# Reordering the builds between the token sums and the channel products of an attention-and-mixer kernel, and its fifth block product

## The chip, the cores and the metric

The kernel runs on one core of a Trainium2 chip. The metric is the device time of one execution in microseconds; three runs of the kernel before gave 585.57, 586.85 and 587.18 us, a median of 586.85. The engines are TensorE (PE: matmuls, with its weight loads, PEld), VectorE (DVE), ScalarE (ACT), GpSimd (POOL) and SyncE (SP), which issues most of the DMAs.

## What is computed

A decay-weighted linear attention over blocks of 64 positions feeds an MLP mixer. Cut to what matters (B = 4, H = 8, S = 768, D = 64; 256 hidden token features, 1536 hidden channel features):

```python
def _attn_ref(q, k, v, lam):
    ...
    for b in range(nb):
        intra = np.einsum('bhic,bhjc->bhij', qb, kb) * Dmask[None]
        intra = np.einsum('bhij,bhjd->bhid', intra, vb)
        inter = np.einsum('bhid,bhde->bhie', qb * lam_pow[None], kv_state)
        out[:, :, sl] = intra + inter
        kv_state = lam_block[None, :, None, None] * kv_state + np.einsum('bhsd,bhse->bhde', kb_dec, vb)
    return out

def _moe_ref(x, w_tok1, w_tok2, w_ch1, w_ch2):
    xt = x.transpose(0, 2, 1)
    h = np.maximum(xt @ w_tok1, 0.0) @ w_tok2
    u = x + h.transpose(0, 2, 1)
    h2 = np.maximum(u @ w_ch1, 0.0) @ w_ch2
    return u + h2
```

The weights arrive as 64-bit floats and are narrowed on the chip.

## The kernel before

**Precision.** Every matmul of the mixer is done three times with operands split into a high part (rounded) and a low part (the remainder): high × high, low × high, high × low. A split is a cast on ACT and a subtraction on POOL or DVE. Narrowing a piece of 64-bit weights is five steps (`narrow`, lines 377 to 395): one on ACT (L382) and four on DVE (L383, L386, L389, L392).

**Attention and token mixing** share one loop over 16 pairs of heads (lines 620 to 704). The token mixing of batch entries 0 to 2 is laid between the attention steps; `take` says how many of the groups each step gets. What is in the list `waiting` is given out by `later`, a few at a time, and `later(99)` empties it. Behind the loop come the last four groups (two token sums of entry 2, two hidden groups of entry 3; lines 713 and 714), then the token sums of entry 3 in four pairs (`token_out_pair`, lines 739 to 742). A pair fills two PSUM banks, and there are two such double banks, so a pair waits until DVE has added the pair before the last (L472).

**Channel mixing** is a list of 24 units, a group of 256 hidden channels (of six) for one batch entry each. First come all groups for the entries 0 and 1, alternating, then the groups backwards for the entries 2 and 3. The first matmul of a unit is a product of 2 × 2 blocks with seven products instead of eight (`mixing`, lines 775 to 825). Its moving operands are made from the four quadrants of u in `build` (line 557): B11, B21 and B22 are quadrants, T1 to T4 come from differences (`t1` to `t4`, DVE). Each operand is split (`part`): the high part by ACT (L582), the low part by DVE if it is named in `on_vector`, else by POOL (L584). `first` holds the operands of entry 0, `parts` those of entry 1. The weights' seven operands are made in `split_c1` (line 525) by eight steps: splits (ACT L374, POOL L375) and four differences on DVE (L534 to L537).

The seven products stand in the order m1, m6, m2, m7, m5, m4, m3. `m1` and `m2` add up in bank `pa`, `m6` and `m7` in `pb`, `m5` and `m3` in `pc`, and `m4` uses `pd`. ACT copies `pa` to `s1` (L788), DVE makes `u2` (L793) and `u3` (L806) from `pb`, `c22` from `pc` (L811), `c21` from `pd` (L817) and `c12` from `pc` (L822). So m7 waits until `u2` has been read from `pb`, and m3 until `c22` has been read from `pc`. The hidden blocks 22, 21 and 12 then go through a relu and a cast on ACT (L771, L772) and a subtraction on POOL (L773); block 11 goes through ACT (L799) and DVE (L800).

The second matmul of a unit is given out as four output pairs (0 to 3, `out_pair`, L835 and L850) in the unit behind it. Pairs 0 and 1 read the hidden blocks 11 and 21, pairs 2 and 3 the blocks 12 and 22. They use the same two double banks in turn. The order of products and pairs in a unit is written out by hand:

```python
    SLOTS = ("m1", "m6", 0, 1, "m2", "m7", 2, "m5", "m4", 3, "m3")
```

**Background work.** `run` (line 1010) counts a product as 6 and a pair as 12. `background(n)` (line 918) lists what else unit n has to do, each with a count from which it is due: weight pieces (`piece_steps`: 0 and 1 belong to the first matmul, 2 and 3 to the second), the steps of `split_c1`, operand builds, fetches of the next 64-bit piece (SP) and `save`, which writes a finished weight group to DRAM with six DMAs (L904), from where the second half of the units gets it back. The raw pieces use two buffers in turn (0 and 2 one, 1 and 3 the other).

All five engines take their instructions in the order in which the code issues them.

Of the kernel before, what the change touches and what calls it, by code (L numbers as in the profile page):

```python
# [22 lines left out]
def kernel(  # L23
# [40 lines left out]
    waiting = deque()  # L64

    def later(n):
        n += len(waiting) > 5
        for _ in range(min(n, len(waiting))):
            waiting.popleft()()
# [25 lines left out]
    NI = len(pairs)  # L95
# [99 lines left out]
    n = 1  # L195
# [177 lines left out]
    def split(hi, lo, src):  # L373
        nc.scalar.copy(out=hi, in_=src)  # L374
        nc.gpsimd.tensor_sub(out=lo, in0=src, in1=hi.bitcast(F32))  # L375
# [146 lines left out]
    def narrow_piece(raw, a, sg):  # L522
        return narrow(raw.rearrange("p (n two) -> p n two", two=2), a, sg)
# [18 lines left out]
    def split_c2(to, i, a):  # L542
        c2h, c2l = to[4:]
        return lambda: split(c2h[:, i - 2], c2l[:, i - 2], a.bitcast(F32))
# [55 lines left out]
    weights = {}  # L600
# [19 lines left out]
    for i in range(-2, NI):  # L620
        if 0 <= i + 1 < NI:
            scores(i + 1)
            scale_q(i + 1)
        if i >= 0:
            outputs(i, 0)
        place = state(i + 1) if 0 <= i + 1 < NI else None
        work = [groups.popleft() for _ in range(take.get(i, 0))]
        if i == NI - 1:
            work.pop(0)()
        if i >= 0:  # L630
            outputs(i, 1)
        if i + 2 < NI:
            turn_q(i + 2)
        if i + 2 < NI:
            if 0 < i + 2 < NP:
                masks(i + 2)
            turns = [(turn_k, 0), (turn_k, 1)] if i + 2 < NKD else []
            if i + 2 < NQ:
                turns += [(turn_q_rows, 0), (turn_q_rows, 1)]
            if i == -2:  # L640
                turns.sort(key=lambda x: x[1])
            for f, g in turns:
                f(i + 2, g)
        if place:
            place()
        later(0 if i == NI - 1 else 1 if work else 2)
        n = early.get(i, len(work) // 4)
        cuts = [0, n, max(n, (3 * len(work) + 1) // 4 if len(work) > 2 else len(work) // 2), len(work)]
        for n in range(3):
            for f in work[cuts[n] : cuts[n + 1]]:  # L650
                f()
                later(2 if len(work) < 3 else 1)
            if n < 2 and i >= 0:
                turn_back(i, n)
                later(1 if work else 2 + n)
            if n == 0 and i + 2 < NI:
                scale_k(i + 2)
        if i == -1:
            load_w1(0)
        if 0 <= i + 3 < NI and i >= -1:  # L660
            load_v(i + 3)
        if i == -1:
            load_w1(1)
        if i + 4 < NI:
            load_kq(i + 4)
        if i == -1:
            load_w1(2)
        if i == 1:
            load_w2()
        if 0 <= i < 3:  # L670
            convert_w1(i)
        if 2 <= i < 4:
            convert_w2(i - 2)
        if i == 3:
            convert_w2(2)
        if i == 5:
            weights[0] = group_tiles(0, False)
            w, w3 = words(2), words(3)
            load_piece(0, 0, w[:, 0:1024])
        if i == 6:  # L680
            load_piece(0, 1, w[:, 1024:2048])
            load_piece(0, 2, w3[:, 1024:2048])
            waiting.extend(narrow_piece(w[:, 0:1024], w3[:, 0:512], w[:, 2048:2560]))
        if i == 7:
            waiting.extend(narrow_piece(w[:, 1024:2048], w3[:, 512:1024], w[:, 2560:3072]))
            waiting.extend(split_c1(weights[0], w3[:, 0:512], w3[:, 512:1024], nc.gpsimd))
            load_piece(0, 3, w3[:, 2048:3072])
        if i == 9:
            waiting.extend(narrow_piece(w3[:, 1024:2048], w3[:, 0:512], w3[:, 512:1024]))
            waiting.append(split_c2(weights[0], 2, w3[:, 0:512]))  # L690
        if i == 10:
            homes[0] = {"B11": (up, None, 1), "B21": (up, None, 1), "T2": (kp, "kn", 2), "T1": (kp, "qn", 2)}
            homes[0] |= {"B22": (kp, "kr", 2), "T3": (kp, "kT", 2), "T4": (kp, "qT", 2)}
            first = build(0, 0, on_vector=("T2", "T1"))
            waiting.extend([first["B11"], first["B21"]])
            waiting.extend(narrow_piece(w3[:, 2048:3072], w3[:, 1024:1536], w3[:, 1536:2048]))
            waiting.append(split_c2(weights[0], 3, w3[:, 1024:1536]))
        if i == 11:
            later(99)
        if i == 13:  # L700
            waiting.extend(first[x] for x in ("t1", "t2", "T2", "T1"))
        if i == NI - 1:
            waiting.extend(first[x] for x in ("t3", "T3", "t4", "T4", "B22"))
    later(99)
    att.close()
    ch = ctx.enter_context(tc.tile_pool(name="ch", bufs=1, reuse_waits="tile"))
# [3 lines left out]
    def temp_of(nm):  # L710
        return cp.tile([P, SB], F32, tag="tmp", bufs=5, name=nm)

    for _ in range(4):
        groups.popleft()()
    p1.close()
    cp = ctx.enter_context(tc.tile_pool(name="cp", bufs=1, side="right", reuse_waits="tile"))
    cs = cp.tile([P, 2560], U32, tag="cs", name="cs")
    narrowed = [cs[:, n * 512 : (n + 1) * 512] for n in range(5)]
    raws = {}

    def fetch(to, x):
        raws[x] = hidp.tile([P, 1024], U32, tag=("hh0", "hl0")[x % 2], name=f"raw{to}{x}")
        load_piece(to, x, raws[x])

    def piece_steps(x):
        return narrow_piece(raws[x], narrowed[x], narrowed[4])

    fetch(1, 0)
    fetch(1, 1)
    steps = {}  # L730
    parts = build(1, 1, on_vector=("T2",))
    pa, pb = piece_steps(0), piece_steps(1)
    order = [
        [parts["t1"], parts["B11"], pa[0], pa[1]],
        [parts["t2"], pa[2], parts["B21"], pa[3]],
        [parts["T2"], pa[4], lambda: fetch(1, 2)],
        [parts["T1"]],
    ]
    for n, fs in enumerate(order):
        token_out_pair(B - 1, n // 2, 2 * (n % 2))  # L740
# [172 lines left out]
        f = cs.bitcast(F32)  # L913
        return [f[:, n * 2 * SB : (n + 1) * 2 * SB].rearrange("p (t s) -> p t s", t=2) for n in range(3)]

    SLOTS = ("m1", "m6", 0, 1, "m2", "m7", 2, "m5", "m4", 3, "m3")

    def background(n):

# [3 lines left out]
        def add(when, *fs):  # L923
            ev.extend((when, f) for f in fs)

        if n == 0:
            c1, pb = steps["c1"], piece_steps(1)
            add(12, pb[0], pb[1], pb[2], c1[0])
            add(36, parts["t3"])
            add(36, parts["T3"])  # L930
            add(36, pb[3], pb[4], lambda: fetch(1, 3))
            add(42, c1[1], parts["t4"])
        if n == 1:
            c1, pa = steps["c1"], piece_steps(2)
            add(6, parts["T4"])
            add(24, c1[2], c1[3], c1[4], c1[5], c1[6], pa[0])
            add(36, parts["B22"])
            add(36, pa[1], pa[2], c1[7])
            add(60, pa[3], pa[4], lambda: fetch(2, 0))
            add(72, split_c2(weights[1], 2, narrowed[2]))  # L940
            add(84, lambda: save(0))
        if 1 < n < NP1 - 1:
            to = g + 1
            if n % 2 == 0:
                pa = piece_steps(3)
                add(12, pa[0], pa[1], pa[2])
                add(24, pa[3], pa[4])
                if n < NP1 - 2:
                    add(24, lambda: fetch(to, 1))
                add(36, split_c2(weights[g], 3, narrowed[3]))  # L950
                if n < NP1 - 2:
                    pb = piece_steps(0)
                    weights[to] = group_tiles(to, to % 2)
                    steps["c1"] = c1 = split_c1(weights[to], narrowed[0], narrowed[1], nc.vector)
                    add(36, pb[0])
                    add(48, pb[1], pb[2])
                    add(72, pb[3], pb[4], lambda: fetch(to, 2))
                    add(84, c1[0])
            else:
                c1, pa, pb = steps["c1"], piece_steps(1), piece_steps(2)  # L960
                add(6, pa[0], pa[1], pa[2])
                add(12, pa[3], pa[4], c1[1], lambda: fetch(to, 3))
                add(36, c1[2], c1[3], c1[4], c1[5], c1[6])
                add(48, c1[7], pb[0], pb[1], pb[2])
                add(72, pb[3], pb[4], split_c2(weights[to], 2, narrowed[2]))
                if to < NG - 1:
                    add(72, lambda: fetch(to + 1, 0))
                if to - 1 < NG - 2:
                    add(84, lambda: save(to - 1))
# [25 lines left out]
        if NP1 + 1 <= n < NP1 + 9:  # L995
            x = n - NP1 - 1
            add(36, lambda: store(x // 4, x % 4))
        if n >= NU - 2:
            x = 2 * (n - NU + 2)
# [25 lines left out]
    for n in range(1, NU):  # L1025
        run(n, [x if isinstance(x, str) else (n - 1, x) for x in SLOTS])
    ytags = deque(("hh1", "hl1"))
# [45 lines left out]
```

## Time and profile before

| What | Value |
|---|---|
| the profiled execution | 586.22 us |
| its span, first to last instruction | 584.4 us |
| mean granted clock of PE | 0.993 |
| first product of unit 0 | at 186.98 us |
| attention and token mixing, before that | 187 us |
| the 24 units and what follows them | 397 us |

The profile is of one execution. A row of a timeline gives the start, the duration, the engine, the line of the kernel, the operation, output and inputs by the names of the tiles, and in square brackets how long the engine had been idle and what it waited for. Several engines work at once, so a row's duration counts towards the end only where another engine waits for it. Starts on one engine may lie up to 0.1 us ahead of the end of the row before, because the instructions are pipelined.

### The profile page before, as it was taken

The page shows a single profiled execution, that of the slowest core. Times are in us where ns is not written, and L with a number is a line of the kernel's source. Part 1 is how long each engine was busy: PE and PEld are TensorE (multiplying, and loading weights), DVE is VectorE, ACT ScalarE, POOL GpSimd, SP SyncE. Part 2 cuts the span into 40 slices and gives each one's busy share as a digit, 9 for nine tenths or more (in the row PEclk, how much of TensorE's full clock was granted, in tenths as well). Part 3 has the DMA queues.
Part 4 walks back from the last instruction along what each step waited for, and adds up shares of the span by engine and source line. Part 5 has one row for each costly group of instructions (what it writes and reads, how often), then busy time and mean ns, then how long its engine had stood idle before and what let it go on. Part 6 is the DMA issues. An engine that isn't in the chain of part 4 may idle for free.

```text
span 584.4 us, 10656 instructions
## 1 busy us (share of the span) xinstructions
PE 558.2 (96%) x4234; PEld 541.1 (93%) x4234; DVE 404.1 (69%) x598; ACT 214.5 (37%) x426; POOL 229.6 (39%) x204
## 2 busy tenths in 40 slices
PE   5998999999999879999999998999999999999995
PEld 4888898999998879999999998999999999999994
DVE  4797887787767887878878888874554454454554
ACT  3564432444244443343444354542212222222221
POOL 6675641745316663345345363541112222222110
PEclk9998999999999989999999999999999999999999
DMA  9999999896002144171727200002434353540237
GB/s 186 255 240 187 179 219 182 157 165 114 2 20 90 37 151 156 42 300 37 271 73 268 75 0 1 0 1 38 144 100 140 97 146 97 153 100 1 40 49 128
DMA packets 176593, 67.81 MB, mean 116 GB/s; under 512 B 163616, under 2 KB 166816, under 8 KB 176544
## 3 DMA queue, kind: packets, MB, share of 16 engines
q1 hardware_dynamic: 173200, 66.05, 46.1%
q10 hardware_dynamic: 3344, 1.09, 0.8%
q8 instruction: 33, 0.54, 0.4%
q14 instruction: 16, 0.13, 0.1%
HBM read 49.29 MB, written 17.83 MB: 115 GB/s over the span
## 4 chain that ended last, share of the span: by engine, by line
PE 81%; DVE 9%; DMA 3%; ACT 3%; issue 2%; POOL 1%; SPq 1%; ACTq 0%; DVEq 0%
PE po L835 30%; PE pc L760 8%; PE pb L760 8%; PE pa L760 7%; PE ph L447 6%; PE pu L484 4%; PE xT L323 4%; PE pd L760 4%; PE sc L299 3%; PE xT L333 3%; DMA vn<-in_v_dram 1%; DMA qn<-in_q_dram 1%; DVE uT L850 1%; PE xp L355 1%; PE kv L265 1%
## 5 line engine op out<-in xcount | busy, mean ns | idle before, releaser
L850 DVE TENSOR_TENSOR uT<-po,uT 128x768 f32<-128x768 f32 x94 | 89.7, 954 | 68.3 <-PE po L835 68.1
L773 POOL TENSOR_TENSOR h22l<-c,h22h 128x384 fp32r<-128x384 f32 x24 | 26.1, 1086 | 166.6 <-ACT h22h L772 166.6
L771 ACT ACTIVATE c<-c 128x384 f32<-128x384 f32 x72 | 37.8, 526 | 128.2 <-DVE c L811 91.3
L286 POOL COPY stb<-sv 64x320 f32<-64x320 f32 x32 | 26.6, 833 | 44.7 <-DVE sv L273 43.8
L773 POOL TENSOR_TENSOR h12l<-c,h12h 128x384 fp32r<-128x384 f32 x24 | 25.1, 1048 | 33.6 <-PE pa L760 19.7
L323 PE MATMUL xT<-a,vn 128*64 128x128 f32 x384 | 37.0, 285 | 1.3 <-ACT uT L340 1.0
L340 ACT COPY uT<-xT 128x384 f32<-128x384 f32 x32 | 15.3, 478 | 56.2 <-PE xT L333 56.2
L793 DVE TENSOR_TENSOR u<-pb,s 128x384 f32<-128x384 f32 x24 | 13.4, 557 | 29.7 <-PE pb L760 19.2
L307 DVE TENSOR_TENSOR a<-sc,mask 128x768 f32<-128x768 f32 x32 | 29.1, 949 | 5.9 <-PE sc L299 5.7
L799 ACT ACTIVATE h11h<-pa 128x384 fp32r<-128x384 f32 x24 | 11.7, 486 | 57.8 <-PE pa L760 57.8
L333 PE MATMUL xT<-qs,stb 128*64 128x128 f32 x320 | 31.8, 277 | 0.0
L447 PE MATMUL ph<-xhi,w1h 128*128 128x256 f32 x96 | 28.2, 294 | 0.8 <-DVE uT L489 0.5
L375 POOL TENSOR_TENSOR c1l<-cs,c1h 128x512 fp32r<-128x512 f32 x15 | 19.6, 1320 | 22.4 <-ACT c1h L374 22.4
L323 PEld LDWEIGHTS xT<-a,vn 128*64 128x64 f32 x384 | 22.6, 139 | 5.5 <-ACT uT L340 2.3
L447 PE MATMUL ph<-xhi,w1l 128*128 128x256 f32 x96 | 27.1, 282 | 0.0
L447 PE MATMUL ph<-xlo,w1h 128*128 128x256 f32 x96 | 27.1, 282 | 0.0
L773 POOL TENSOR_TENSOR h21l<-c,h21h 128x384 fp32r<-128x384 f32 x24 | 26.1, 1088 | 1.8 <-ACT h21h L772 1.0
L299 PE MATMUL sc<-qT,kT 64*128 64x128 f32 x384 | 26.3, 284 | 0.2 <-ACT qT L237 0.2
L299 PEld LDWEIGHTS sc<-qT,kT 64*128 64x128 f32 x384 | 23.3, 192 | 3.3 <-issue 1.8
L364 DVE TENSOR_TENSOR xlo<-xp,xhi 128x384 fp32r<-128x384 f32 x32 | 17.7, 552 | 11.4 <-ACT xhi L363 11.3
L252 POOL TENSOR_TENSOR qs<-qT,lamp 128x640 f32<-128x640 f32 x16 | 25.3, 1583 | 0.3
L835 PE MATMUL po<-h12h,c2h 128*128 128x384 f32 x64 | 21.8, 341 | 0.0
(271 smaller groups left out, 1894.7 us busy)
## 6 DMA issues: line engine op xcount, KB each, us to landing
raw<-in_moe_w_ch_dram SPq DMA_DIRECT2D x20, 512.0 KB, 3.9
vn<-in_v_dram SPq DMA_DIRECT2D x16, 384.0 KB, 5.4
kn<-in_k_dram SPq DMA_DIRECT2D x30, 192.0 KB, 4.5
out_dram<-y SPq DMA_DIRECT2D x110, 48.0 KB, 1.8
qn<-in_q_dram SPq DMA_DIRECT2D x44, 96.0 KB, 3.3
kr<-in_k_dram SPq DMA_DIRECT2D x32, 96.0 KB, 2.9
dc1h<-c1h SPq DMA_DIRECT2D x4, 768.0 KB, 5.4
dc1l<-c1l SPq DMA_DIRECT2D x4, 768.0 KB, 6.7
```

Source lines behind the costliest of these rows:

```text
L252: nc.gpsimd.tensor_mul(out=qss[i], in0=qTs[i][:, P:].rearrange("p (c i) -> p c i", i=P), in1=lamp[:, p, None, :].broadcast_to([P, NC - 1, P]),
L286: nc.gpsimd.tensor_copy(out=st[r, :, h, :], in_=sv[r].rearrange("p (e c) -> p c e", c=NC - 1))
L299: nc.tensor.matmul(out=sc[h][:, c * P : (c + 1) * P], lhsT=kTs[i][r, cs], rhs=qTs[i][r, cs], start=True, stop=True,)
L307: nc.vector.tensor_mul(out=a, in0=pair.rearrange("p h (c i) -> p h c i", i=P), in1=mask[:, 2 * p : 2 * p + 2, None, :].broadcast_to([P, 2, ...
L323: nc.tensor.matmul(out=xT[h * D : (h + 1) * D, cs], lhsT=vns[i][:, h, c, :], rhs=weights_of[i, g, h][:, cg, :], start=(cg == 0), stop=False,)
L333: nc.tensor.matmul(out=xT[h * D : (h + 1) * D, cs], lhsT=st[:, c - 1, h, :], rhs=qss[i][:, c - 1, :], start=False, stop=(cg == 2),)
L447: nc.tensor.matmul(out=ph, lhsT=w[:, c, fs], rhs=x[:, c], start=(i == 0), stop=(i == 3 * NC - 1))
L760: nc.tensor.matmul(out=to, lhsT=w[:, t], rhs=x[:, t], start=(start and i == 0), stop=(i == 5), skip_group_check=not start,)
L771: nc.scalar.activation(src, src, AF.Relu)
L773: nc.gpsimd.tensor_sub(out=hl, in0=src, in1=hh.bitcast(F32))
L835: nc.tensor.matmul(out=to, lhsT=w[:, jj, t * P : (t + 1) * P], rhs=h, start=(i == 0), stop=(i == 3 * JG - 1))
L850: nc.vector.tensor_add(out=ub, in0=po, in1=ub)
```

## The change

Four things are altered, and no work is added or left out.

- In every unit but the first, the fifth product stands directly behind the seventh, ahead of output pair 2.
- The builds t3, T3, t4, T4 and B22 of the first operand no longer come at the end of the attention loop; they stand between the last four groups of token work, and their low parts move from POOL to DVE. B11 and B21 of the second operand come up from the pairs of token sums to the same place. T3 of the second operand moves to DVE.
- The steps of weight piece 0, piece 1 and the second operand's remaining builds are spread over the pairs and the units 0 and 1 in another order.
- Weight piece 2 of group 1, with the fetch behind it and its split, moves from unit 1 to the beginning of unit 2. Its fetch then stands behind `save(0)` on SP's queue.

```diff
-            first = build(0, 0, on_vector=("T2", "T1"))
+            first = build(0, 0, on_vector=("T1", "T2", "T3", "T4", "B22"))
...
-        if i == NI - 1:
-            waiting.extend(first[x] for x in ("t3", "T3", "t4", "T4", "B22"))
...
-    for _ in range(4):
+    parts = build(1, 1, on_vector=("T2", "T3"))
+    order = [[first["t3"], parts["B11"]], [first["T3"]], [first["t4"], parts["B21"]], [first["T4"], first["B22"]]]
+    for fs in order:
         groups.popleft()()
+        for f in fs:
+            f()
...
-        return narrow_piece(raws[x], narrowed[x], narrowed[4])
+        return [lambda k=k: narrow_piece(raws[x], narrowed[x], narrowed[4])[k]() for k in range(5)]
...
-    parts = build(1, 1, on_vector=("T2",))
-    pa, pb = piece_steps(0), piece_steps(1)
+    pa = piece_steps(0)
     order = [
-        [parts["t1"], parts["B11"], pa[0], pa[1]],
-        [parts["t2"], pa[2], parts["B21"], pa[3]],
-        [parts["T2"], pa[4], lambda: fetch(1, 2)],
-        [parts["T1"]],
+        [parts["t1"], pa[0]],
+        [parts["t2"], pa[1]],
+        [pa[2], parts["T2"], parts["T1"]],
+        [pa[3], pa[4], lambda: fetch(1, 2)],
     ]
...
-    SLOTS = ("m1", "m6", 0, 1, "m2", "m7", 2, "m5", "m4", 3, "m3")
+    SLOTS = ("m1", "m6", 0, 1, "m2", "m7", "m5", 2, "m4", 3, "m3")
...
         if n == 0:
             c1, pb = steps["c1"], piece_steps(1)
-            add(12, pb[0], pb[1], pb[2], c1[0])
-            add(36, parts["t3"])
-            add(36, parts["T3"])
-            add(36, pb[3], pb[4], lambda: fetch(1, 3))
-            add(42, c1[1], parts["t4"])
+            add(12, pb[0], pb[1], c1[0])
+            add(24, pb[2])
+            add(36, parts["t3"], parts["T3"])
+            add(42, pb[3], pb[4], lambda: fetch(1, 3), c1[1])
         if n == 1:
-            c1, pa = steps["c1"], piece_steps(2)
-            add(6, parts["T4"])
-            add(24, c1[2], c1[3], c1[4], c1[5], c1[6], pa[0])
-            add(36, parts["B22"])
-            add(36, pa[1], pa[2], c1[7])
-            add(60, pa[3], pa[4], lambda: fetch(2, 0))
-            add(72, split_c2(weights[1], 2, narrowed[2]))
+            c1 = steps["c1"]
+            add(12, parts["t4"])
+            add(24, parts["T4"], c1[2], c1[3], c1[4], c1[5])
+            add(36, c1[6], parts["B22"])
+            add(48, c1[7])
             add(84, lambda: save(0))
         if 1 < n < NP1 - 1:
             to = g + 1
             if n % 2 == 0:
+                if n == 2:
+                    pc = piece_steps(2)
+                    add(6, *pc, lambda: fetch(2, 0), split_c2(weights[1], 2, narrowed[2]))
                 pa = piece_steps(3)
```

## The prediction

> **What bounds the kernel now.** I read the page first, then the waits of TensorE (PE), then windows and the chain of waits at the places which those named, and last the timelines of the engines there.
>
> ```profile
> span 584.4 us, 10656 instructions
> ...
> PE 558.2 (96%) x4234; PEld 541.1 (93%) x4234; DVE 404.1 (69%) x598; ACT 214.5 (37%) x426; POOL 229.6 (39%) x204
> ```
>
> PE is busy for 558.2 of 584.4 us, so only its holes can be won: no matmul is added or removed. The profiled execution took 586.22 us around this span; the median of the three runs, 586.85, is 0.63 above it, and I carry differences over unchanged. The columns of the next view are total us, times, longest.
>
> ```profile
> PE pc L760 <- DVE c L811: 6.2, 3, 3.9
> ...
> PE pb L760 <- DVE u L793: 1.7, 1, 1.7
> PE pu L467 <- DVE uT L472: 1.4, 1, 1.4
> ```
>
> All three wait for VectorE (DVE) to empty a PSUM bank: the third product (into `pc`) for `c22`, the seventh for `u2`, a pair of token sums for the sums two pairs earlier. The hole of 3.9 us stands at the end of unit 1, and it costs more than itself (the windows' columns are length, busy time of PE, PEld, DVE, ACT and POOL, granted clock, DMA share and GB/s; the chain's start and length):
>
> ```profile
> 190.00:195.00 5.00, 3.35 (x19) 3.08 (x18) 4.38 (x8) 0.87 (x3) 0.72 (x1) 1.00 0.18 61
> ...
> 215.00:220.00 5.00, 4.92 (x21) 4.95 (x22) 1.98 (x4) 4.45 (x9) 3.89 (x4) 0.71 1.04 421
> ```
>
> ```profile
> 215.08 2.26 PE pc L760 x6
> 217.34 1.36 PE pa L760 x6
> ...
> 233.51 1.06 PE pa L760 x6
> ...
> 235.63 4.16 PE po L835 x24
> ```
>
> A product takes 1.06 us and two output pairs 4.16, so a unit without a hole is 7 × 1.06 + 2 × 4.16 = 15.74 us. Behind the hole the clock is 0.71, and two products take 2.26 + 1.36 instead of 2.12: 1.5 us more. Against no waits at all, 3.9 + 1.5 + 1.7 + 1.4, and 6.2 − 3.9 = 2.3 in the other two waits on `c22`, make 10.8 us: the most that can be won.
>
> **What makes DVE late.**
>
> ```profile
> 179.24 1.84 POOL L584 TENSOR_TENSOR B11l<-uT,B11h 128x768 fp32r<-128x768 f32 x1
> ...
> 171.72 0.95 DVE L574 TENSOR_TENSOR th<-uT 128x768 f32<-128x768 f32 x1
> ...
> 180.08 1.81 DVE L574 TENSOR_TENSOR th<-uT 128x768 f32<-128x768 f32 x1
> ...
> 173.46 1.01 DVE L489 TENSOR_TENSOR uT<-pu,uT 128x384 f32<-128x384 f32 x2
> 173.68 1.86 POOL L584 TENSOR_TENSOR T3l<-th,T3h 128x768 fp32r<-128x768 f32 x1 [12.46 <-issue]
> ```
>
> The same difference takes 0.95 us alone, and 1.81 when it begins while GpSimd (POOL) works: it ends 181.89, which is 0.81 behind POOL's end at 181.08. So a DVE instruction on SBUF alone waits out a POOL one; DVE's additions from PSUM at 173.46 did not. This decides every step below.
>
> **Part 1: the first operand's builds among the token sums.** T3, T4 and B22 leave POOL (3 × 1.86 us) for DVE (3 × 0.95), behind token sums instead of ahead of them; B11 and B21 of the second operand come up from the pairs to between them, still on POOL.
>
> ```profile
> 170.73 0.48 ACT L363 CAST xhi<-xp 128x384 fp32r<-128x384 f32 x1 [0.17 <-PE xp L355]
> 172.70 0.84 ACT L582 CAST T3h<-th 128x768 fp32r<-128x768 f32 x1 [1.49 <-DVE th L574]
> ...
> 171.41 0.33 PE L484 MATMUL pu<-w2l,hh 128*128 128x384 f32 x1
> ...
> 176.93 0.34 PE L467 MATMUL pu<-w2h,hh 128*128 128x384 f32 x1
> ...
> 176.72 0.42 DVE L452 SCALAR_TENSOR_TENSOR hl<-ph,hh 128x256 fp32r<-128x256 f32 x1 [2.25 <-ACT hh L451]
> ...
> 184.79 0.44 PE L467 MATMUL pu<-w2h,hh 128*128 128x384 f32 x1 [1.45 <-DVE uT L472]
> ```
>
> In the new order: ScalarE (ACT) casts B11h from 171.2 to 172.0, and POOL has B11l until 173.9. DVE adds the token sum (171.8 to 172.3), so t3 comes just behind POOL and ends 174.7; next sum 175.2; the cast of T3 (0.84) ends 175.6, T3l 176.6, `hl` 176.9. POOL takes B21l (176.8 to 178.6), t4 waits it out: 179.4; second `hl` 179.7, cast of T4 180.2, T4l 181.2, B22l 182.1. Only then comes the first pair's addition, until 183.0. The third pair needs that bank; PE, which starts the pairs at 176.93 as now, is there at 181.1 (two pairs at 2.08). A new wait of 1.9 us, in place of the 1.45 at the fourth pair, which starts at 185.1 against 184.79: no gain. Should t4 or t3 come ahead of POOL (0.1 to 0.2 us decide), the addition ends at 182.2 or 181.4.
>
> ```profile
> 187.28 1.84 POOL L584 TENSOR_TENSOR T1l<-th,T1h 128x768 fp32r<-128x768 f32 x1 [3.70 <-ACT T1h L582]
> 187.33 2.60 DVE L584 TENSOR_TENSOR T2l<-tl,T2h 128x768 fp32r<-128x768 f32 x1
> ...
> 191.33 0.54 DVE L793 TENSOR_TENSOR u<-pb,s 128x384 f32<-128x384 f32 x1
> ...
> 191.92 0.45 PE L760 MATMUL pb<-T3h,c1h 128*128 128x384 f32 x1 [1.65 <-DVE u L793]
> ...
> 196.22 0.33 PE L760 MATMUL pa<-B11h,a11h 128*128 128x384 f32 x1
> ```
>
> From the end of that addition DVE's line to `u2` is, by starts 0.08 us ahead of the end before: t1, sum and t2 at 0.87, the piece's first step 0.35, a sum 0.87, a step 0.6, 4.4 us in all (the steps' 0.41 and 0.69 stand in a fence below); there T2l and POOL's T1l meet. If T1l is first, as at 187.28, T2l ends at 7.1, and a sum, two steps and `u2` follow: 9.4. If T2l is first, T1l ends at 7.1, the sum runs beside it, and only the two steps and `u2` follow: 8.6. The seventh product of unit 0 begins between 181.4 + 8.6 = 190.0 and 183.0 + 9.4 = 192.4; I take 191.4, nearest the row of now, 191.92. **Gain 0.5 us** (−0.5 to +1.9). The fifth, fourth and third product follow; unit 1 begins 4.2 us later, at 195.6 (now 196.22).
>
> **Part 2: unit 1.** It loses piece 2 (five steps, its split, a fetch) and T3's products on POOL; t4 and T4 move into it from unit 0's end and unit 1's start.
>
> ```profile
> 204.08 2.05 DVE L534 TENSOR_TENSOR cs<-cs 128x256 f32<-128x256 f32 x1 [0.71 <-POOL c1l L375]
> 206.16 0.43 DVE L535 TENSOR_TENSOR cs<-cs 128x256 f32<-128x256 f32 x1
> ...
> 209.40 2.22 DVE L386 SCALAR_TENSOR_TENSOR cs<-raw,cs 128x512 uint32<-128x512 uint32 x1
> ...
> 213.33 0.41 DVE L389 TENSOR_SCALAR cs<-cs 128x512 f32<-128x512 f32 x1
> 213.78 0.69 DVE L392 SCALAR_TENSOR_TENSOR cs<-cs 128x512 uint32<-128x512 uint32 x1
> 214.38 0.55 DVE L811 TENSOR_TENSOR c<-pc,u 128x384 f32<-128x384 f32 x1
> ```
>
> Piece 2's DVE steps (the second at 209.40 to the last, which ends 214.4) stand right ahead of the `c22` that PE waits for, and that one no longer has them, nor the second pair's addition, ahead of it. What is left I count from unit 1's start, with 1.3 us for a split of 512 columns on POOL, an estimate between 1.02 (384 columns, `h21l` in a fence below) and 1.84 (768). `c12` of unit 0 ends at 3.8 (T3l waits out `h21l` ahead of it), piece 1's last two steps at 4.8, the split's cast on ACT at 5.5, `s1` and `u2` at 6.5. t4 waits out the split on POOL (to 7.3): 8.1. The first pair's addition ends at 9.0, T4's cast too. Now c1's four differences (0.43 each) and T4l meet: T4l ends at 11.3 if it gets in behind the first of them, at 12.6 if behind the fourth; the fourth product is there at 11.6. In the first case the second pair's addition ends at 13.3 and `c22`, three short instructions later, at 15.4; in the second at 13.4; the third product is there at 14.7. B22l has a split and T4l ahead of it on POOL: 15.7 to 16.0, wanted at 15.1. So some 0.9 us of waiting stays, on the operands T4 and B22 (0 to 2.0). Unit 2 begins at 195.6 + 15.74 + 0.9 = 212.2 (210.0 to 214.4), now 217.34: **5.1 us with part 1**, 3.0 to 7.4.
>
> By the Trainium skill (TensorE: Matmul & The Clock Gate, Part 1) PE falls to half its clock after about 3.4 us of idleness, so new waits of up to 2.1 us would cost no clock; the row of 190 to 195 us, with a hole of 1.65 and a clock of 1.00, agrees. If they did cost it, the 1.5 us would come back, and the sum by that would be 582.8.
>
> **Part 3: unit 2 takes piece 2.** Four DVE steps (2 × 0.41 + 2 × 0.69 = 2.2 us) and one on ACT come ahead of `u2`. ACT comes to its step at 3.0 behind unit 1's `c12` and `s1`, the last two steps on DVE follow it, and `u2` ends at 5.1; the seventh product wants it at 2.12 + 4.16 + 1.06 = 7.3. PE's two pairs hide it: nothing, and if DVE comes over 2.2 us later than I count, each us beyond costs one. On SP's queue the fetch for raw tile 0 now stands behind the save of group 0, not ahead of it.
>
> ```profile
> 212.12 0.46 SPq L904 DMA_DIRECT2D da11h<-a11h  x1
> ...
> 215.19 1.15 SPq L904 DMA_DIRECT2D dc2l<-c2l  x1
> ```
>
> The save waits for nothing new, so it goes out once the fetch ahead of it is issued, near 195 us instead of 212, and is over long before. The fetch goes out 3.6 us into unit 2; were it to take 6 us, the reader on ACT, wanted at 6.3, would hold back the cast of `h11`, which has 9 us until its use: nothing.
>
> **Part 4: the fifth product ahead of the second pair, in 22 units.** PE does the same work; the third product now comes 5.3 us behind the fifth, not 3.2. It pays only where DVE is late, in units 10 and 11.
>
> ```profile
> 358.80 0.96 DVE L584 TENSOR_TENSOR T3l<-cs,T3h 128x768 fp32r<-128x768 f32 x1
> 359.68 0.55 DVE L811 TENSOR_TENSOR c<-pc,u 128x384 f32<-128x384 f32 x1
> ...
> 360.28 0.44 PE L760 MATMUL pc<-B22h,c1h 128*128 128x384 f32 x1 [1.47 <-DVE c L811]
> ...
> 362.50 1.02 POOL L773 TENSOR_TENSOR h21l<-c,h21h 128x384 fp32r<-128x384 f32 x1
> ```
>
> `c22` goes ahead of two of the three instructions before it and is done at 358.3, before it is needed: the 1.47 us go. But ACT's relu and cast of `c22` (two passes over half the columns of T3's cast, 0.84: some one us, an estimate) now stand ahead of T3's cast, and T3l ahead of `c21`; `h21l` then ends at 364.1, not 363.5, while PE comes 1.5 us earlier to the pair that reads it. It waits there instead. Of the 2.3 us of both units I keep **0.4** (−0.3 to 2.3).
>
> Sum: 5.1 + 0.4 = 5.5 us; 586.22 − 5.5 = 580.7 for the profiled execution, **581.3** for the median. The bounds together: 7.4 + 2.3 = 9.7 (577.1) and 3.0 − 0.3 = 2.7 (584.1).
>
> **Rivals.**
>
> *All waits go.* Every near tie with POOL falls DVE's way and `h21l` is in time: 577.1. For it: three ties within 0.2 us; against it: they would all have to. Chance 0.14.
>
> *The hole stays in unit 1.* c1's chain, T4 and B22 share POOL and DVE there; if the operands come 3 us later than I count, PE again waits over 3 us and loses clock. Without any wait unit 2 would begin 6.0 us earlier (217.34 − 195.6 − 15.74); less 3.9 + 1.5, plus part 4's 0.4, is 1.0 us gained: 585.8. For it: my margins are under 1 us; against it: six us of DVE work leave the unit. Chance 0.13.
>
> *DVE becomes the bound: slower.* Four differences move from POOL to DVE, 4 × 0.95 = 3.8 us. If DVE then runs without a hole from the token sums to unit 2, the waits only change places, and the 3.8 come on top: 590.6. It decides if DVE idles for less than these 3.8 us there.
>
> ```profile
> 175.00:180.00 5.00, 5.00 (x36) 5.00 (x35) 1.64 (x3) 3.51 (x6) 4.92 (x4) 1.00 0.46 179
> ```
>
> Against it: DVE is busy for 1.64 of these 5 us, just where three of the four go. Chance 0.07.
>
> **How the numbers follow.** My forecast has 0.66 and its bounds 577.1 to 584.1; the range 577.0 to 585.5 takes in the best case and a part of the third, and leaves out under 2 in 10. A measurement here can tell 0.3% (1.8 us) from no change, so faster means under 585.1: 0.66 + 0.14 and a little of the third, 0.81; the same 0.12; slower 0.07.
>
> **What would show it.** Right: no wait on L811 above 1 us; unit 2 beginning near 212; new waits of 1 to 2 us at the third pair of token sums and at the seventh product of unit 0; the window behind unit 1 at clock 1.00; a wait on an operand (`h21l`) after unit 10. Wrong: a hole over 3 us anywhere before unit 2, waits in unit 2 itself, or a pair that waits for the moved fifth product in the steady units.

## The result and the profile after

The changed kernel takes **582.61 us** in the median (582.14 to 583.82), the kernel before 586.85 (585.57 to 587.78): 4.2 us or 0.65% less, a ratio of 0.9935 with a 95% interval of 0.9915 to 0.9954. The profiled execution took 582.14 us, its span 580.4 against 584.4. In the changed code the lines past 725 stand one further down: L761 is the L760 of before, L794 the L793, L812 the L811, L836 the L835.

The head of the page:

```profile
span 580.4 us, 10666 instructions
...
PE 557.8 (96%) x4234; PEld 538.9 (93%) x4234; DVE 407.6 (70%) x602; ACT 215.9 (37%) x426; POOL 222.9 (38%) x200
```

PE does the same work in the same time, and 4.0 us of holes are gone. DVE has 3.5 us more and POOL 6.7 less: the four low parts that changed engines, dearer on POOL.

The waits of PE (total us, times, longest):

```profile
PE pu L467 <- DVE uT L472: 1.9, 1, 1.9
...
PE pb L761 <- DVE u L794: 0.9, 1, 0.9
...
PE po L836 <- ACT h21h L773: 0.7, 1, 0.7
PE po L836 <- DVE uT L851: 0.7, 3, 0.3
PE po L836 <- POOL h21l L774: 0.5, 1, 0.5
...
PE pc L761 <- DVE c L812: 0.3, 1, 0.3
```

The 6.2 us of waits for `c22` have become 0.3. What was not there before is the three rows on `po`, 1.9 us together: output pairs that wait for block 21 and for DVE's additions.

Two windows of the same stretches as before (length, busy time of PE, PEld, DVE, ACT, POOL, granted clock, DMA):

```profile
190.00:195.00 5.00, 4.11 (x24) 3.79 (x23) 4.11 (x8) 1.10 (x3) 1.04 (x2) 1.00 0.06 25
...
215.00:220.00 5.00, 5.00 (x30) 5.00 (x29) 4.59 (x7) 1.99 (x4) 2.65 (x2) 1.00 0.40 107
```

Behind unit 1 the clock is 1.00 where it was 0.71, and PE gets 30 matmuls into those 5 us instead of 21.

**Where the time came from**, by the first matmul of each unit in the two timelines, before minus after: −0.5 us at unit 0 (186.98, 187.50), +0.3 at unit 1 (196.22, 195.95), **+4.8** at unit 2 (217.14, 212.33), +5.2 at unit 3 and through to unit 10 (343.73, 338.55), then +6.65 at unit 11 (361.43, 354.78), +5.0 at unit 12 (378.33, 373.30), +4.5 at unit 13 (394.09, 389.63) and still 4.5 at the last matmul (578.64, 574.16). So all of the gain is made in unit 1 and the restart behind it, and 0.7 us are given back in units 10 to 12. Half a microsecond more goes behind the last matmul: from its start to the end of the span it is 5.8 us before and 6.2 after, though the last output is sent off 1.8 us behind it in both. Over the profiles of all runs this end takes 6.05 to 6.25 us where the first operand's builds are moved, and 5.74 to 5.82 where they aren't (before, m5_alone, piece2_alone, builds_undone). So it goes with the builds' move; by what way isn't known.

### The profile page after: what moved, and what is told of

It is laid out like the page before. It is cut to its first block, busy times and chain, and to the rows that moved or that the text cites. A ratio compares the mean times of both kernels' runs of the same rounds, so it can differ in the third digit from the quotient of the medians.

```text
span 580.4 us, 10666 instructions
## 1 busy us (share of the span) xinstructions
PE 557.8 (96%) x4234; PEld 538.9 (93%) x4234; DVE 407.6 (70%) x602; ACT 215.9 (37%) x426; POOL 222.9 (38%) x200
## 5 line engine op out<-in xcount | busy, mean ns | idle before, releaser
L774 POOL TENSOR_TENSOR h21l<-c,h21h 128x384 fp32r<-128x384 f32 x24 | 27.9, 1162 | 31.9 <-ACT h21h L773 25.2
L794 DVE TENSOR_TENSOR u<-pb,s 128x384 f32<-128x384 f32 x24 | 13.4, 557 | 28.7 <-PE pb L761 17.2
L836 PE MATMUL po<-h21h,c2h 128*128 128x384 f32 x64 | 21.6, 338 | 0.7 <-ACT h21h L773 0.7
```

What stands on the lines that cost most here:

```text
L774: nc.gpsimd.tensor_sub(out=hl, in0=src, in1=hh.bitcast(F32))
L836: nc.tensor.matmul(out=to, lhsT=w[:, jj, t * P : (t + 1) * P], rhs=h, start=(i == 0), stop=(i == 3 * JG - 1))
```

## Experiments

**Theory:** piece 2's steps on DVE stood right ahead of the `c22` that PE waited for; taking them out of unit 1 is the gain, the new place of m5 adds nothing to it, and the builds' move is worth little. **Rivals:** m5's new place closes the hole, since it lets `c22` come 2.1 us later; or the builds do, since they clear DVE and POOL for unit 1. A second question is why units 10 to 12 lose, a third what in POOL's work holds DVE up.

The end of the attention stage moves by about 1 us between profiles of the same code: the first pair of token sums begins between 175.92 and 176.93 us in before, m5_alone and piece2_alone, and between 176.22 and 177.11 in after, m5_undone and t3_later. So stages are compared from that first pair's matmul. "To unit 2" is the time from it to unit 2's first matmul, "units 10–12" that from unit 10's to unit 13's; both come from the timeline of PE in the one profiled execution. A ratio compares a kernel with the runs of before that were made beside it (their medians lie between 586.42 and 586.85), not with the first row.

| Kernel | to unit 2 | units 10–12 | median us | ratio to before (95%) |
|---|---|---|---|---|
| before | 40.21 | 50.36 | 586.85 | |
| after | 35.50 | 51.08 | 582.61 | 0.9935 (0.9915–0.9954) |
| m5_alone | 37.57 | 51.04 | 584.88 | 0.9980 (0.997–0.999) |
| piece2_alone | 36.08 | 50.34 | 580.91 | 0.9918 (0.9903–0.9934) |
| builds_undone | 36.19 | 51.07 | 581.72 | 0.9923 (0.9909–0.9938) |
| m5_undone | 36.22 | 50.33 | 582.42 | 0.9938 (0.9923–0.9954) |
| t3_later | 36.94 | 50.44 | 582.84 | 0.9934 (0.9920–0.9948) |
| lock_write_only | 33.48 | 51.08 | 580.31 | 0.9895 (0.9878–0.9911) |
| lock_write_timed | 33.50 | 51.03 | 579.51 | one execution |
| sums_first | 33.94 | 51.05 | 579.92 | 0.9887 (0.9871–0.9903) |
| both | 33.94 | 50.43 | 579.96 | 0.9891 (0.9875–0.9908) |
| spread | 33.95 | 49.64 | 579.46 | 0.9879 (0.9861–0.9896) |
| sums_first_m5_undone | 34.63 | 50.33 | 580.52 | 0.9897 (0.9881–0.9913) |

### Which part carries the gain

**m5_alone**: the kernel before with nothing but the new order of products.

```diff
-    SLOTS = ("m1", "m6", 0, 1, "m2", "m7", 2, "m5", "m4", 3, "m3")
+    SLOTS = ("m1", "m6", 0, 1, "m2", "m7", "m5", 2, "m4", 3, "m3")
```

> The kernel before with one edit: the fifth product stands behind the seventh. First theory (c22 is late in unit 1 because of what DVE does ahead of it): c22 now goes ahead of the second pair's addition and of piece 2's last two steps and ends near 213.0 instead of 214.9, so the hole at the third product shrinks from 3.9 to about 2.0 us, the clock stays at 1.00 behind it, and unit 2 begins near 214.2 instead of 217.1; units 10 to 12 lose about 0.7 us on the wait for h21l. In all about 2.2 us faster, 584.6. Rival (the order of the products does the whole): 582.6. Rival (it only pays together with the moved piece): the hole stays over 3 us, 586.8.

The timeline of PE in m5_alone, at the end of unit 1 and in unit 2:

```profile
212.39 0.41 PE L760 MATMUL pc<-B22h,c1h 128*128 128x384 f32 x1 [2.23 <-DVE c L811]
...
216.68 0.44 PE L835 MATMUL po<-h21h,c2h 128*128 128x384 f32 x1 [0.36 <-ACT h21h L772]
...
217.76 0.45 PE L835 MATMUL po<-h21l,c2h 128*128 128x384 f32 x1 [0.47 <-POOL h21l L773]
```

The hole shrinks from 3.9 to 2.23 us, and with it went the drop of the clock: 2.6 us by unit 2. But unit 2 then takes 17.20 us instead of the changed kernel's 15.85, because `h21` is late for the pair in it, and units 10 to 12 lose 0.7. What remains at the end is 0.2% (584.88). The new order does soften the hole, but it doesn't carry the change.

**piece2_alone**: the kernel before with piece 2, its fetch and its split moved to unit 2, and nothing else.

```diff
-        return narrow_piece(raws[x], narrowed[x], narrowed[4])
+        return [lambda k=k: narrow_piece(raws[x], narrowed[x], narrowed[4])[k]() for k in range(5)]
...
-            c1, pa = steps["c1"], piece_steps(2)
+            c1 = steps["c1"]
             add(6, parts["T4"])
-            add(24, c1[2], c1[3], c1[4], c1[5], c1[6], pa[0])
+            add(24, c1[2], c1[3], c1[4], c1[5], c1[6])
             add(36, parts["B22"])
-            add(36, pa[1], pa[2], c1[7])
-            add(60, pa[3], pa[4], lambda: fetch(2, 0))
-            add(72, split_c2(weights[1], 2, narrowed[2]))
+            add(36, c1[7])
...
+                if n == 2:
+                    pc = piece_steps(2)
+                    add(6, *pc, lambda: fetch(2, 0), split_c2(weights[1], 2, narrowed[2]))
```

> The kernel before with one edit: weight piece 2, its fetch and its split move from unit 1 to the beginning of unit 2. First theory: DVE has 4.4 us less ahead of c22 in unit 1, which ends near 212.3; the third product waits about 1.1 us, the clock stays at 1.00, unit 2 begins near 213.4, and units 2 and 3 have no wait: 583.1. Rival (the work only moves on): a wait of 2 to 4 us appears in unit 2 or 3, 586 to 588.

The timeline of PE in piece2_alone, unit 1's third product and unit 10's:

```profile
210.86 0.41 PE L760 MATMUL pc<-B22h,c1h 128*128 128x384 f32 x1 [0.72 <-DVE c L811]
...
354.79 0.44 PE L760 MATMUL pc<-B22h,c1h 128*128 128x384 f32 x1 [1.47 <-DVE c L811]
```

This one move brings the whole gain. The hole is 0.72, and the two stages take 36.08 + 50.34 = 86.42 us against 86.58 in the changed kernel. The median is 580.91, 2.2 below what I expected, and 1.7 below the full change too. In the profiles, whose spans are 1.5 us apart, 0.9 of that is an attention stage that ended earlier, 0.2 the two stages and 0.4 the end behind the last matmul. The 1.47 at unit 10 stays, as in every kernel here with the old order of products, and costs less than what took its place.

**builds_undone**: the changed kernel with the first operand's builds back at the end of the loop on POOL, and B11 and B21 back among the pairs.

```diff
-            first = build(0, 0, on_vector=("T1", "T2", "T3", "T4", "B22"))
+            first = build(0, 0, on_vector=("T2", "T1"))
...
+        if i == NI - 1:
+            waiting.extend(first[x] for x in ("t3", "T3", "t4", "T4", "B22"))
...
-        [parts["t1"], pa[0]],
-        [parts["t2"], pa[1]],
+        [parts["t1"], parts["B11"], pa[0]],
+        [parts["t2"], parts["B21"], pa[1]],
```

> The changed kernel with the first operand's t3, T3, t4, T4 and B22 back at the end of the attention loop (low parts on POOL) and the second operand's B11 and B21 back among the pairs. First theory: the wait at the third pair of token sums (1.9 us) goes, DVE waits out POOL's B11l and B21l between the pairs instead, and unit 1 begins within 0.5 us of 195.95: 582.6, within 0.5. Rival (the builds among the last token sums carry the gain): 584.5 or more.

The timeline of PE in builds_undone, unit 0's seventh product:

```profile
190.83 0.44 PE L760 MATMUL pb<-T3h,c1h 128*128 128x384 f32 x1 [2.69 <-DVE u L793]
```

Its windows there:

```profile
188.00:191.00 3.00, 0.31 (x2) 0.17 (x2) 2.96 (x6) 0.66 (x2) 0.18 (x1) 1.00 0.16 63
191.00:194.00 3.00, 3.00 (x13) 3.00 (x14) 1.82 (x4) 0.14 (x1) 0.70 (x1) 0.67 0.00 0
194.00:197.00 3.00, 3.00 (x15) 3.00 (x14) 1.72 (x3) 1.58 (x4) 1.02 (x1) 0.76 0.84 214
```

The wait among the token sums is gone and one of 2.69 us stands at m7 instead; the granted clock falls to 0.67 and 0.76 behind it. The two stages take 87.26 us, 0.7 more than in the changed kernel, with that drop in them, and the median, 581.72, is not above the changed kernel's: the builds' move shifts a wait from one place to another (and goes with the 0.5 us at the end, which is 5.74 us here). The rival that they carry the gain falls.

**m5_undone**: the changed kernel with the old `SLOTS` (the first diff backwards).

> The changed kernel with the old order of products and pairs. First theory: c22 of unit 1 is 0.9 us later, behind the second pair's addition, so the third product waits about 0.5 us and unit 2 begins near 212.8; in units 10 and 11 the waits on c22 of 1.5 and 0.8 us come back and the waits on h21l (0.7 and 0.5) go, so unit 13 begins about 0.2 us earlier or later than in the changed kernel: 582.4, no difference that can be told. Rival (the order of the products carries the gain): 585 to 587.

The timeline of PE in m5_undone, the third product of the units 1, 10 and 11:

```profile
211.29 0.41 PE L761 MATMUL pc<-B22h,c1h 128*128 128x384 f32 x1 [0.44 <-DVE c L812]
...
355.21 0.44 PE L761 MATMUL pc<-B22h,c1h 128*128 128x384 f32 x1 [1.47 <-DVE c L812]
...
372.10 0.44 PE L761 MATMUL pc<-B22h,c1h 128*128 128x384 f32 x1 [0.82 <-DVE c L812]
```

Unit 1 loses 0.7 us (17.09 instead of 16.38), units 10 to 12 win 0.75: 582.42 against 582.61. With piece 2 out of the way, m5's new place nets nothing.

### What holds DVE up: POOL's reading or its writing

**lock_write_only** and **lock_write_timed**: in the changed kernel, POOL's two subtractions for B11 and B21 of entry 1 become memsets of the same tiles, so these two operands lose their low parts. The second one holds the memsets back behind a small copy by ACT and issues three, to fill the time that the subtraction took.

```diff
+            if b == 1 and o in ("B11", "B21"):
+                nc.scalar.copy(out=lo[:, :, 0:8], in_=src[:, :, 0:8])
+                nc.gpsimd.memset(lo.bitcast(F32), 0.0)
+                nc.gpsimd.memset(lo.bitcast(F32), 0.0)
+                nc.gpsimd.memset(lo.bitcast(F32), 0.0)
+                return
```

(lock_write_only has one memset and no copy.)

> The changed kernel in which POOL writes zeros for the low parts of B11 and B21 of entry 1 in place of the two subtractions, so these low parts are left out of the products: POOL works at the same places, but reads nothing from SBUF. Theory (a DVE instruction with two SBUF inputs waits out a POOL instruction that reads SBUF): t3 and t4 take 0.95 us, not 2.49 and 2.50, the first pair's addition ends about 2 us earlier, the wait at the third pair (1.92) goes, unit 0's seventh product begins near 189.5: 580.6. Rival (any POOL instruction holds DVE up): t3 and t4 stay over 1.5 us each, 582 or more.

> As lock_write_only (the low parts of B11 and B21 of entry 1 are left out, POOL writes zeros), with the zeros held until ACT has cast the high part, and written three times, so that POOL works for some 2.2 us at the very place of its subtraction and reads nothing. Theory (only a POOL instruction that reads SBUF holds up a DVE instruction with two SBUF inputs): t3 and t4 still take 0.95 us. Rival (any POOL instruction does): over 1.5 us each, the wait at the third pair of token sums is back at 1.5 to 2 us.

In lock_write_only t3 and t4 took 0.95 us each and the wait at the third pair was gone, but with nothing to hold them the memsets ran near 162 us, long before, so it shows only that POOL's subtractions were the cause. lock_write_timed puts them in place. Its timelines of POOL and of DVE:

```profile
171.56 0.74 POOL L586 MEMSET B11l<- 128x768 f32 x1 [10.94 <-issue]
172.36 0.74 POOL L587 MEMSET B11l<- 128x768 f32 x1
...
175.63 0.74 POOL L586 MEMSET B21l<- 128x768 f32 x1 [1.73 <-ACT B21l L585]
...
171.66 0.95 DVE L574 TENSOR_TENSOR th<-uT 128x768 f32<-128x768 f32 x1
...
175.13 0.95 DVE L596 TENSOR_TENSOR tl<-tl,uT 128x768 f32<-128x768 f32 x1
```

t3 begins 0.10 us behind a memset and runs beside it and the next, t4 has one begin in its midst, and both take 0.95 us, the time alone. Beside a subtraction that reads two tiles the same instructions take 2.49 and 2.50 (below). So a POOL instruction that reads SBUF holds DVE up, and one that only writes it doesn't. The Trainium skill (SBUF — State Buffer, Who interferes with whom) says just that: a DVE instruction with two SBUF inputs contends with a GpSimd instruction that reads SBUF, not with one that only writes. These rows agree. (A subtraction and a memset differ in more than the reading, and a POOL instruction that reads a single tile was not tried.)

### The waits that stood in the changed kernel

**t3_later**: the second wait is taken at its supposed cause. The operand build T3 of the units 10 and 11 is put behind `c21`, so that its cast and its subtraction don't stand ahead of `h21`; in unit 10, T1 moves back with it.

```diff
-            add(60, bl["T3"])
-            add(72, bl["T1"])
-            add(84, bl["B21"])
+            add(72, bl["T3"])
+            add(84, bl["T1"], bl["B21"])
...
-            add(72, bl["t3"], bl["T3"])
+            add(72, bl["t3"])
+            add(84, bl["T3"])
```

> The changed kernel with two builds due later: T3 of entry 2 in unit 10 at 72 and T1 at 84 (were 60 and 72), T3 of entry 3 in unit 11 at 84 (was 72). First theory (the moved fifth product puts the relu and cast of c22 ahead of T3's cast on ACT, T3l ahead of c21 on DVE, and so delays h21l): the waits on h21h and h21l at unit 11's first pair (0.73 and 0.52 us) and on the pairs' additions (0.20 and 0.33) fall under 0.2 us each, unit 13 begins about 2 us earlier than in the changed kernel: 580.4. Rival (DVE's total work in units 10 to 12 is the bound, whatever its order): the waits move to the third products of units 11 and 12, 582.6.

The waits for `h21` did go. The timelines of DVE and PE in unit 11 of t3_later show what came:

```profile
360.56 2.17 DVE L584 TENSOR_TENSOR T1l<-cs,T1h 128x768 fp32r<-128x768 f32 x1
362.65 0.55 DVE L823 TENSOR_TENSOR c<-pc,u 128x384 f32<-128x384 f32 x1
...
364.73 0.44 PE L761 MATMUL pa<-B21h,c1h 128*128 128x384 f32 x1 [1.69 <-ACT s L789]
```

T1's low part, now later, takes 2.17 us on DVE and stands ahead of `c12`. On ACT `s1` stands behind the relu and the cast of `c12`, so PE waits 1.69 us for `s1`. I had expected 580.4; 0.6 us are won in those units, and the median, 582.84, is no better than the changed kernel's (in its profile the clock fell as well, below). The cause of the old wait was right; the cure only moved the late work.

**sums_first**: the first wait, at the third pair of token sums. T4 and B22 move behind the first pair, the second operand's t1 behind the second, and the end of piece 0 with its fetch into unit 0.

```diff
-    order = [[first["t3"], parts["B11"]], [first["T3"]], [first["t4"], parts["B21"]], [first["T4"], first["B22"]]]
+    order = [[first["t3"], parts["B11"]], [first["T3"]], [first["t4"], parts["B21"]], []]
...
-        [parts["t1"], pa[0]],
-        [parts["t2"], pa[1]],
+        [first["T4"], first["B22"], pa[0]],
+        [parts["t1"], parts["t2"], pa[1]],
         [pa[2], parts["T2"], parts["T1"]],
-        [pa[3], pa[4], lambda: fetch(1, 2)],
+        [],
...
-            add(12, pb[0], pb[1], c1[0])
-            add(24, pb[2])
+            add(12, *steps["p0"][3:], lambda: fetch(1, 2), pb[0], pb[1], c1[0])
+            add(30, pb[2])
```

> The changed kernel with T4 and B22 of the first operand behind the first pair of token sums, t1 behind the second, and piece 0's last two steps with their fetch behind the sixth product of unit 0 (piece 1's third step behind its fifth product). First theory (the waits at the third pair and at unit 0's seventh product come from the order on DVE): the wait of 1.92 us goes, that of 0.89 falls to about 0.5, unit 1 begins near 194.1 instead of 195.95, and as unit 1 hangs on DVE by the same distances the 1.8 us stay: 580.8. Rival (DVE's sum of work up to unit 2 is the bound): the time comes back as waits in units 0 and 1, 582.5.

The timeline of PE in sums_first has no wait at the third pair, and at m7 and m3 of unit 0:

```profile
188.76 0.45 PE L761 MATMUL pb<-T3h,c1h 128*128 128x384 f32 x1 [0.37 <-DVE u L794]
...
192.67 0.44 PE L761 MATMUL pc<-B22h,c1h 128*128 128x384 f32 x1 [0.49 <-DVE c L812]
```

Of the 1.92 + 0.89 = 2.81 us of waits ahead of unit 1, 0.86 are left; 1.6 us are won on the way to unit 2, and the median is 579.92, 0.9 better than expected. Those waits were time on the path.

**both** (t3_later and sums_first together), **sums_first_m5_undone** (sums_first with the old `SLOTS`), and **spread**, which is sums_first with the builds of the units 10 to 12 laid out otherwise:

```diff
-            add(60, bl["T3"])
-            add(72, bl["T1"])
             add(84, bl["B21"])
+            add(90, bl["T3"])
...
-            add(6, al["t4"])
+            add(6, al["T1"], al["t4"])
...
-            add(24, bl["t1"], bl["B11"])
+            add(24, bl["t1"])
...
-            add(72, bl["t3"], bl["T3"])
+            add(72, bl["t3"])
+            add(90, bl["T3"])
...
+            add(6, bl["B11"])
```

> The edits of the two runs before last and last in this call together (T3 and T1 later in units 10 and 11; T4 and B22 behind the first pair, piece 0's last steps into unit 0). First theory: their gains of about 2.2 and 1.8 us add, 578.6. Rivals: 580.4 or 580.8 if only one of them holds, 582.5 if neither.

> The kernel of the run sums_first with the old order of products and pairs. First theory: the third product of unit 1 waits about 0.5 us for c22, units 10 to 12 take 0.7 us less: 579.7, no difference that can be told. Rival (the moved fifth product pays once the other waits are gone): 581 or more.

> The kernel of the run sums_first with the builds of units 10 to 12 spread otherwise: T3 of entry 2 behind unit 10's third product, its T1 into unit 11 behind the first product, T3 of entry 3 behind unit 11's third product, B11 of entry 3 into unit 12. First theory (the waits of units 10 to 12 come from casts and differences that stand ahead of c21, s1 and the pairs' additions): c21 and s1 are in time, no wait over 0.4 us stays there, units 10 to 12 take about 48 us instead of 51.1, 577.2. Rival (DVE's sum of work is the bound there): the waits move on into units 11 to 13, 579.5 to 580.5.

both adds nothing to sums_first (579.96): T1's place costs in unit 11 what it did in t3_later. spread takes units 10 to 12 from 51.08 to 49.64 us and has the lowest median, 579.46 (ratio 0.9879 to before), but 2.3 above what I expected, since waits of 0.69 at m7 and 0.21 at m3 came up; between spread (578.12 to 580.00) and sums_first (579.63 to 580.26) the times don't decide. sums_first_m5_undone again moves 0.7 us from one stage to the other (34.63 + 50.33 = 84.96 us against 84.99 in sums_first); its median, 580.52, lies between the 579.7 expected and the rival's 581, and doesn't decide by itself. Both spread and sums_first beat the changed kernel and the one before.

## Why the prediction was right, and where it missed

Forecast 581.3, measured 582.6: the sign, the place and the main term held; the term of part 4 had the wrong sign.

**DVE waits out POOL (part 1): right, to 0.2 us.** The timelines of POOL, DVE and PE in the changed kernel:

```profile
171.98 1.84 POOL L584 TENSOR_TENSOR B11l<-uT,B11h 128x768 fp32r<-128x768 f32 x1 [10.86 <-issue]
...
176.59 1.84 POOL L584 TENSOR_TENSOR B21l<-uT,B21h 128x768 fp32r<-128x768 f32 x1 [2.77 <-ACT B21h L582]
...
172.16 2.49 DVE L574 TENSOR_TENSOR th<-uT 128x768 f32<-128x768 f32 x1
...
176.76 2.50 DVE L590 TENSOR_TENSOR tl<-tl,uT 128x768 f32<-128x768 f32 x1
...
182.22 0.95 DVE L472 TENSOR_TENSOR uT<-pu,uT 128x768 f32<-128x768 f32 x1
...
187.49 0.95 DVE L584 TENSOR_TENSOR T2l<-tl,T2h 128x768 fp32r<-128x768 f32 x1
...
187.50 2.65 POOL L584 TENSOR_TENSOR T1l<-th,T1h 128x768 fp32r<-128x768 f32 x1 [9.06 <-ACT T1h L582]
...
183.22 0.44 PE L467 MATMUL pu<-w2h,hh 128*128 128x384 f32 x1 [1.92 <-DVE uT L472]
...
191.69 0.44 PE L761 MATMUL pb<-T3h,c1h 128*128 128x384 f32 x1 [0.89 <-DVE u L794]
```

t3 ends at 174.65 (forecast 174.7), t4 at 179.26 (179.4), the first pair's addition at 183.17 (183.0), and the wait at the third pair is 1.92 (1.9). At the tie of T2l with T1l DVE came first by 0.01 us, one of the two cases that I had carried. m7 began at 191.69, forecast 191.4: a gain of 0.2, not 0.5, of which 0.1 came from the attention stage.

**Unit 1 (part 2): right in size, the operand named was another.** The timelines of PE and of SP's queue:

```profile
195.95 0.33 PE L761 MATMUL pa<-B11h,a11h 128*128 128x384 f32 x1
...
208.95 0.44 PE L836 MATMUL po<-h12h,c2h 128*128 128x384 f32 x1 [0.19 <-DVE uT L851]
...
212.33 0.34 PE L761 MATMUL pa<-B11h,a11h 128*128 128x384 f32 x1
...
194.69 0.42 SPq L905 DMA_DIRECT2D da11h<-a11h  x1
...
215.81 4.57 SPq L515 DMA_DIRECT2D raw<-in_moe_w_ch_dram  x2
```

Unit 1 lost 212.33 − 195.95 − 15.74 = 0.6 us where I had kept 0.9, and not on T4 or B22, which were in time, but at the fourth pair's bank: 0.19 by its row and 0.27 for the stop (below), with some 0.2 that I did not place. Unit 2 began at 212.33 (212.2), and the clock behind it stayed at 1.00, so 5.17 us were won by unit 3, of 5.1 forecast. That it is so close is partly luck. Unit 1 began 0.35 us later than forecast and waited 0.3 less. And the 217.34 that I took from the chain for unit 2's start before is 217.14 in the timeline, while I left out that the low clock still cost 0.36 us in unit 2 (16.21 us before, 15.85 after).

**Piece 2 in unit 2 (part 3): right.** No wait in units 2 to 9; the save went out at 194.69 (forecast near 195) and the fetch at 215.81.

**Part 4 is the term that was mis-sized**: +0.4 forecast with a low end of −0.3, **−0.7 measured**. The timelines of ACT, DVE, PE and POOL at the turn of units 10 and 11:

```profile
354.17 0.51 ACT L773 CAST h22h<-c 128x384 fp32r<-128x384 f32 x1
354.59 0.83 ACT L582 CAST T3h<-cs 128x768 fp32r<-128x768 f32 x1
...
355.45 1.14 DVE L584 TENSOR_TENSOR T3l<-cs,T3h 128x768 fp32r<-128x768 f32 x1 [1.01 <-ACT T3h L582]
356.52 0.54 DVE L818 TENSOR_TENSOR c<-u,pd 128x384 f32<-128x384 f32 x1
...
357.21 0.34 PE L836 MATMUL po<-h11l,c2h 128*128 128x384 f32 x1
358.27 0.45 PE L836 MATMUL po<-h21h,c2h 128*128 128x384 f32 x1 [0.73 <-ACT h21h L773]
358.56 0.34 PE L836 MATMUL po<-h21h,c2l 128*128 128x384 f32 x1
...
359.42 0.44 PE L836 MATMUL po<-h21l,c2h 128*128 128x384 f32 x1 [0.52 <-POOL h21l L774]
...
372.15 0.44 PE L761 MATMUL pc<-B22h,c1h 128*128 128x384 f32 x1 [0.27 <-DVE c L812]
```

The chain is the one forecast: `c22` goes first on ACT, T3's cast waits for it, T3l for the cast, `c21` for T3l, and the pair that reads `h21` waits. The 1.47 us did go (unit 11 began with a lead of 6.65). But I reckoned with one such wait and none of its echoes, and I priced a wait at its row. Matmuls here start 0.174 us apart (a row of 0.34 us overlaps the next by 0.16); from 357.21 to 358.56 are two starts and 1.35 us, so 1.00 us is lost where the row says 0.73. That holds for every stop in these units: its row and 0.27 more, because the start behind it is 0.28 later, not 0.17, and 0.16 goes before the row begins. Over units 10 to 12 the starts that come late add up to 3.76 us in the changed kernel (waits of 0.73, 0.52, 0.20, 0.27 and 0.33, and a stop without a row) and to 3.01 before (1.47, 0.79, and two short stops): the 0.7 us that were lost. By the rows alone the waits fell, from 2.26 to 2.05 us; that there are more of them makes the loss. For the same reason the 10.8 us of the prediction, the most that could be won, is too low by 0.2 to 0.3 us for each of its five waits. t3_later bears the chain out: T3 put behind `c21` takes both `h21` waits away.

The row of the 0.79 in the kernel before, in its timeline of PE:

```profile
377.17 0.44 PE L760 MATMUL pc<-B22h,c1h 128*128 128x384 f32 x1 [0.79 <-DVE c L811]
```

**The clock: right here, wrong as a rule.** I took it that new waits of up to 2.1 us cost no clock. In the changed kernel's profile they didn't (1.00 behind the 1.92). In t3_later the same code at the same place gave this, in the timeline of PE and in the windows:

```profile
183.51 0.45 PE L467 MATMUL pu<-w2h,hh 128*128 128x384 f32 x1 [1.91 <-DVE uT L472]
```

```profile
183.00:186.00 3.00, 2.49 (x11) 2.49 (x12) 3.00 (x5) 0.00 (x0) 0.00 (x0) 0.77 0.00 0
186.00:189.00 3.00, 3.00 (x13) 3.00 (x13) 2.52 (x5) 1.56 (x2) 1.22 (x1) 0.66 0.00 0
```

From first pair to unit 0 it took 12.27 us there against 10.67 in the changed kernel: 1.6 us for a clock that fell (matmuls 0.32 us apart for a while, not 0.174). m5_undone, with the same code there too, waited 1.91 us and kept 1.00. The changed kernel's own times fit that, but not strictly: 582.14 and 582.61 at mean clocks of 0.998 and 0.995, 583.80 and 583.82 at 0.992 and 0.990, and between them 582.56 at 0.993. That these are the same drop isn't shown, since only one of those executions has a profile.

So of the 1.5 us between the 5.5 forecast and the 4.0 measured in the span, 1.1 are part 4 and 0.5 the end behind the last matmul, to which the prediction gave no term; up to unit 3 it was 5.2 against 5.1. The rivals fell: no hole over 2 us stayed in unit 1, DVE did not become the bound, and not all waits went.

## What to carry to other kernels

Look at what stands right ahead of the late instruction on its engine, and move that to where the engine has slack; here one such move, of five steps and a fetch, was worth as much as the whole change. An order that brings one result forward pushes another behind it on every engine that it is moved past: follow the pushed one to its reader, and the reader's successor too, and price several small waits above one of the same length. Where two engines contend, first ask which of them reads: here an instruction of POOL that read SBUF held DVE's up, and one that only wrote it did not.

## What the runs showed of the hardware

- The length of a hole alone doesn't decide whether PE's clock falls. Behind 3.93 us (before) it was 0.71 and behind 2.69 (builds_undone) 0.67; behind 2.23 (m5_alone), 1.92 (after) and 1.91 (m5_undone) it stayed at 1.00, and behind 1.91 in the same code (t3_later) it was 0.66 to 0.77. The Trainium skill (TensorE: Matmul & The Clock Gate, Part 1) gives an idle window of about 3.4 us that runs free of the program. That the outcome varies between executions agrees with a free-running window; that 1.91 us of idleness suffices doesn't agree with its length.
- A stop of PE in a row of 128x384 matmuls cost 0.27 us beyond the idle time of its row, in each of the stops of the units 10 to 12, however short the row.
